# Turning the output weights first, loading them back early, and issuing the middle loop's stores and weight loads from GpSimd

## The chip, the cores and the metric

The kernel runs on one core of one Trainium2 chip. The metric is the device time of one execution in microseconds (us), on the slowest core, which here is the only one.

## The reference, cut to what matters

The program computes a transformer block and all its gradients: `x + A(layernorm(x)) + B(layernorm(x))`, and the vector-Jacobian product for `grad_out`.

```python
def _A_ref(x, mem0, Wq, Wk, Wv, Wo, seg_len):      # S = 2048, D = 512, 32 heads of 128, M = 8, seg = 32
    mem = mem0
    for s in range(n_seg):                         # 64 segments, one after the other
        h = concatenate([mem, xs], axis=1)         # 8 memory rows + 32 rows of the segment
        q, k, v = h @ Wq, h @ Wk, h @ Wv
        o = softmax(mask(q k^T * scale)) v
        o = einsum('bhte,hed->btd', o, Wo)
        mem = o[:, :M, :]                          # the next segment needs this one's output
        ...
def _B_ref(x, w1, b1, w2, b2):                     # F = 1792
    h = x @ w1 + b1
    out = relu(h)**2 @ w2 + b2
```

Because `mem` runs from segment to segment, the kernel has a serial chain of 64 segments forward and a serial chain of 64 segments backward. The backward chain needs the weights transposed: `WoT` (4 MiB), and `WT` for q, k and v (12 MiB).

## The kernel before

The kernel has five stages: the dense part B, the forward chain (to about 1220 us), a **middle loop** of 16 steps, the backward chain, and the weight gradients. The change touches the seam between the two chains.

During the forward chain TensorE (PE) turns two heads of one weight per segment, and a store puts them into scratch in HBM. The order is Wq, Wk, Wv, Wo, so Wo is finished by the last segment.

```python
            t, h0 = divmod(2 * s, H)               # t: 0 = Wq, 1 = Wk, 2 = Wv, 3 = Wo
            def wt():                              # 8 transposes of one step, on PE
                ps["wt"] = fr.tile([P, 8 * P], BF16, name="ps_wt", tag="r")
                ...
            o["ws"] = lambda: dma(S_WOT[...] if t == 3 else S_WT[...], st["wt"][:]...)   # cut
```

At the end of the forward chain the room of Wq, Wk and Wv is freed, and `WoT` is loaded into it. `dma` issues from SyncE (SP), `pdma` from GpSimd. Around it on SP stand the last transposing DMAs of the forward chain and their stores (`OC`, `ON`, `S_ON`).

```python
        def load_back():
            wq_cm.__exit__(None, None, None)
            wk_cm.__exit__(None, None, None)
            ...
            dma(back["WoT"][:], S_WOT[:])          # 4 MiB
```

The middle loop handles the part of the backward pass that does not depend on the chain. One step `b` of it uses loads made a step earlier, and also carries a piece of the dense weight gradients (`ps_w`, from `wA` and `wB`) to keep PE busy. The names with a minus sign belong to the step before.

```python
    LB_ORDER = ("o0mm o1mm qp0- o0ev o1ev qp1- qea0- qeb0- W1- ld o0fl o1fl o0te o1te s0 s1 qea1- qeb1- "
                "d10 d20 d30 d40 so- x0- tu0 d11 d21 d31 d41 tu1 W0 v1- x1- v0").split()
    with sb("ls", 2) as ls, ...:                   # l_gON and the other step tiles have two buffers
            def ld():
                if b + 1 < NB:
                    load(b + 1)                    # l_vTM, l_vTL, l_P, l_kM, l_kL: about 1.1 MiB
                chunk(b + 1)                       # wB: 1 MiB, in runs of 512 bytes
                for t, h in pieces[b:b + 1]:       # 12 pieces, steps 0 to 11
                    dma(WT[t][:, h:h + 8, :], S_WT[:, t, h:h + 8, :])      # 1 MiB
            o["o%dev" % p] = lambda p=p: acp(T["gON"][:, HC[p]], ps["o", p][:])   # ScalarE writes l_gON
            def so():
                dma(S_GOL[b], T["gON"][:])         # this store frees l_gON
                dma(S_GSL[b], T["gS"][:])
                dma(S_GQL[b], T["gq"][:])
        def store(b, i, ps):
            if b < NCH:
                dma(out_9[fc * P:(fc + 1) * P, :], ps["wt", i][:])
            else:
                ...
                    dma(out_7[dc * P:(dc + 1) * P, f0:f0 + CH], ps["wt", i][:, x * CH:(x + 1) * CH])
```

Everything in this excerpt goes through SP's one queue, in this order: loads, `wB`, `WT`, then the stores.

## Time and profile before

| | before |
|---|---|
| time, median of 3 runs | 3210.66 us (3199.31 to 3212.24) |
| profiled execution | 3213.6 us |
| head: start of the last `ps_wt` transposes to the eviction of loop step 1 | 77.3 us |
| loop: eviction of step 1 to that of step 15 | 248.1 us |
| handover: to the first `gv` eviction of the backward chain | 29.9 us |
| backward chain, first to last `gv` eviction | 973.2 us |

"Eviction" is ScalarE's (ACT's) copy of `ps_proj` into `l_gON`; it happens at the same place in every step and makes a good clock.

The first view is part 2 of the profile page of the kernel before: the span in 40 slices of 80.3 us, busy tenths of PE, granted clock of PE, busy tenths of the DMA engines, and the rate (the rows of the other engines are left out).

```profile
PE   7996999999999883657688888888988848999998
PEclk9998999999999996888899999999999978999999
DMA  9447467767677667887468666767766699999993
GB/s 260 161 129 265 142 173 196 197 188 190 169 189 193 166 171 213 233 246 211 124 173 191 162 159 187 171 159 184 183 162 175 164 239 197 216 184 216 187 184 88
```

The dip of PE from the 16th to the 19th slice (3, 6, 5, 7) is the seam. Elsewhere PE stands at 6 tenths or more, apart from a 4 before the last stage, and the change does not reach there.

Next, stretches of the kernel before. Columns: window, its length, busy time of PE, PE's weight loads, VectorE, ACT and GpSimd (with instruction counts), then granted clock, DMA share and GB/s. The first is the loop, the second one step of the backward chain.

```profile
1295.70:1543.80 248.10, 167.73 (x2987) 102.13 (x2996) 66.40 (x154) 53.30 (x125) 0.00 (x0) 0.86 0.80 229
1926.02:1943.98 17.96, 14.75 (x398) 7.35 (x398) 6.77 (x20) 5.44 (x15) 5.11 (x9) 0.90 0.71 234
```

In the loop neither PE (168 of 248 us) nor the DMA engines (0.80) are full. Something makes them wait for each other. The waits of the kernel before between 1280 and 1560 us say what (total us, times, longest):

```profile
PE l_pp L516 <- ACT l_gq L372: 69.7, 15, 14.5
ACT l_gON L372 <- DMA S_GOL<-l_gON: 69.7, 12, 15.4
...
PE ps_w L1024 <- DMA wB<-S_AN: 4.4, 1, 4.4
```

ACT waits 69.7 us for the store that frees `l_gON`, and PE waits as long for a copy queued behind it on ACT. The chain of waits of the kernel before shows why that store is late. Columns: start, length, what.

```profile
1354.94 5.20 PE ps_w L1024 x15
1360.14 0.24 PE ps_tr L165 x4
1360.38 0.16 SPq L1007
1360.54 0.05 issue
1360.59 1.99 SPq L955
1362.58 0.05 issue
1362.63 8.29 DMA S_GOL<-l_gON
...
1371.51 0.59 ACT l_gON L372
```

It reads as a loop. PE's `ps_w` matmuls free `wB`; then SP may issue the next `wB` (L1007) and `WT` (L955); only behind these comes `S_GOL`, and it lands 8.3 us later, though it is only 256 KiB. Then ACT writes `l_gON`, and PE goes on, to the next `ps_w`. So the store waits in two lines: in SP's program, behind an issue that must wait for PE, and in the queue, behind 2 MiB of loads. A step takes 18.6 us on average from step 1 to step 12.

The head has its own stall. The first view is SP's waits between 1220 and 1290 us, the second SP's timeline (start, length of the issue, instruction), both of the kernel before.

```profile
SPq L742 <- DMA S_ON<-OC: 9.5, 1, 9.5
```

```profile
1223.13 1.43 SPq L671 DMA_TRANSPOSE OC<-OT  x1
1224.60 3.44 SPq L530 DMA_DIRECT2D vM<-S_A  x4
1228.14 0.39 SPq L898 DMA_DIRECT2D WoT<-S_WOT  x1
...
1229.25 0.61 SPq L673 DMA_DIRECT2D S_ON<-OC  x1
...
1244.49 1.30 SPq L742 DMA_TRANSPOSE ON<-OTL  x1
```

`S_ON` stands behind the 4 MiB of `WoT`, and the transpose of `ON` must wait for it. A serial row of transposes and stores follows and ends with the first load of `wA` at 1274.1 us.

### The profile page before, as it was taken

Reading aid. Unit: us, or ns where it says so; the run is one execution under the profiler, and the core shown is the slowest. Engines: PE = TensorE matmul, PEld = TensorE weight load, DVE = VectorE, ACT = ScalarE, POOL = GpSimd, SP = SyncE. Lnnn points to the kernel's source line nnn. Section 1 sums busy time; section 2 is a strip of 40 time slices with the busy share of each in tenths; the row PEclk is TensorE's granted clock in tenths of the full one; section 3 lists DMA queues with packets and bytes.
Section 4 is the critical chain, followed back from the end, with each engine's and each line's share of the span. In section 5 each row is a group of like instructions: output and inputs, shape, how many; then the busy total and the mean of one; then the engine's idle time right before and its main releaser. Section 6 shows DMA issues by size and latency. Waiting matters only on the chain.

```text
span 3213.6 us, 115334 instructions
## 1 busy us (share of the span) xinstructions
PE 2726.7 (85%) x51522; PEld 1409.3 (44%) x51672; DVE 1259.6 (39%) x3515; ACT 1011.8 (31%) x2356; POOL 328.5 (10%) x601
## 2 busy tenths in 40 slices
PE   7996999999999883657688888888988848999998
PEld 4453455555544441325444444444444423444443
DVE  5542565655655552222344444444444400100001
ACT  2332454444444441112233333333333201111111
POOL 0000000000000000000122222222222100000000
PEclk9998999999999996888899999999999978999999
DMA  9447467767677667887468666767766699999993
GB/s 260 161 129 265 142 173 196 197 188 190 169 189 193 166 171 213 233 246 211 124 173 191 162 159 187 171 159 184 183 162 175 164 239 197 216 184 216 187 184 88
DMA packets 853923, 594.40 MB, mean 185 GB/s; under 512 B 595745, under 2 KB 735666, under 8 KB 850226
## 3 DMA queue, kind: packets, MB, share of 16 engines
q1 hardware_dynamic: 836018, 532.47, 67.0%
q0 software_dynamic: 17408, 54.54, 5.9%
q8 instruction: 405, 6.64, 0.9%
q14 instruction: 92, 0.75, 0.1%
HBM read 205.14 MB, written 250.10 MB: 142 GB/s over the span
## 4 chain that ended last, share of the span: by engine, by line
PE 58%; DMA 13%; SPq 12%; DVE 6%; ACT 5%; issue 5%; POOL 0%; ACTq 0%; POOLq 0%; DVEq 0%
PE ps_proj L388 12%; PE ps_gR L429 9%; PE ps_gw L1441 8%; SPq L1366 6%; PE b_pp L516 4%; PE ps_sum L438 3%; PE ps_R L429 3%; PE ps_tr L165 2%; DMA S_GOL<-l_gON 2%; DMA out_dram<-wt 2%; PE ps_RL L1145 2%; PE ps_L L346 2%; PE ps_sc L409 1%; PE ps_w L1024 1%; PE f_pp L516 1%
## 5 line engine op out<-in xcount | busy, mean ns | idle before, releaser
L1441 PE MATMUL ps_gw<-gn,HNc 128*128 128x512 bf16 x1881 | 417.4, 381 | 9.0 <-ACT wt L1416 6.9
L1441 PEld LDWEIGHTS <-HNc 128*128 128x128 bf16 x1920 | 188.5, 98 | 233.2 <-issue 11.3
L372 ACT CAST f_N<-ps_proj 128x512 bf16<-128x512 f32 x384 | 218.3, 586 | 183.9 <-PE ps_proj L388 163.3
L1416 ACT CAST wt<-ps_gw 128x512 bf16<-128x512 f32 x126 | 69.2, 592 | 558.3 <-DMA out_dram<-wt 357.5
L388 PEld LDWEIGHTS <-X 128*32 128x32 bf16 x6144 | 159.0, 97 | 171.2 <-issue 16.4
L1399 DVE TENSOR_TENSOR gx<-ps_rows,gb 128x512 f32<-128x512 f32 x16 | 11.1, 691 | 427.3 <-PE ps_rows L1397 427.3
L1441 PE MATMUL ps_gw<-GOc,gn 128*128 128x512 bf16 x627 | 142.0, 386 | 28.5 <-DMA gn<-S_ON 27.7
L429 PE MATMUL ps_gR<-WT,gv 128*32 128x512 bf16 x2048 | 150.4, 387 | 9.7 <-ACT gOT L372 4.4
L429 PE MATMUL ps_gR<-WT,gk 128*32 128x512 bf16 x2048 | 145.6, 405 | 12.2 <-issue 5.3
L429 PE MATMUL ps_gR<-WT,gq 128*32 128x512 bf16 x2048 | 142.2, 404 | 3.7 <-issue 3.7
L388 PE MATMUL ps_proj<-Wk,X 128*32 128x512 bf16 x2048 | 133.5, 393 | 9.7 <-ACT dN L372 4.8
L388 PE MATMUL ps_proj<-Wq,X 128*32 128x512 bf16 x2048 | 130.4, 385 | 7.1 <-DVE X L451 6.5
L388 PE MATMUL ps_proj<-WoT,GT 128*32 128x512 bf16 x2048 | 123.9, 384 | 7.7 <-POOL GT L1175 6.5
L372 ACT CAST gON<-ps_proj 128x512 bf16<-128x512 f32 x128 | 74.9, 585 | 168.9 <-PE ps_proj L388 168.9
L429 PE MATMUL ps_R<-Wo,OT 128*32 128x512 bf16 x2048 | 123.3, 382 | 0.5 <-DVE OT L375 0.4
L388 PE MATMUL ps_proj<-Wv,X 128*32 128x512 bf16 x2048 | 121.5, 378 | 0.0
L438 PE MATMUL ps_sum<-identF,R 128*128 128x128 f32 x512 | 101.7, 299 | 22.4 <-ACT R L372 16.1
L796 POOL COPY kM<-f_kT 128x256 bf16<-128x256 bf16 x64 | 25.6, 401 | 834.7 <-DVE f_kT L375 834.7
L372 ACT CAST gk<-b_pp 128x256 bf16<-128x256 f32 x192 | 65.9, 382 | 142.7 <-PE b_pp L516 134.9
L1441 PEld LDWEIGHTS <-gn 128*128 128x128 bf16 x640 | 63.6, 99 | 105.7 <-DMA gn<-S_ON 28.0
L465 DVE TENSOR_TENSOR ds_t<-ps_sc,l_P 128x256 f32<-128x256 f32 x32 | 12.9, 405 | 216.7 <-PE ps_sc L409 216.7
L438 PEld LDWEIGHTS ps_sum<-identF,R 128*128 128x128 f32 x512 | 56.5, 144 | 84.4 <-ACT R L372 59.1
(229 smaller groups left out, 4849.4 us busy)
## 6 DMA issues: line engine op xcount, KB each, us to landing
S_A<-f_N SPq DMA_DIRECT2D x64, 512.0 KB
out_dram<-wt SPq DMA_DIRECT2D x142, 128.0 KB
S_A<-f_N SPq DMA_DIRECT2D x64, 256.0 KB
S_ON<-OC SPq DMA_DIRECT2D x64, 256.0 KB
b_qN<-S_A POOLq DMA_DIRECT2D x64, 256.0 KB, 3.9
b_kN<-S_A POOLq DMA_DIRECT2D x64, 256.0 KB, 3.8
S_GB<-gv SPq DMA_DIRECT2D x32, 512.0 KB
S_GB<-gq SPq DMA_DIRECT2D x32, 512.0 KB
```

What stands on the lines that cost most here:

```text
L165: nc.tensor.transpose(ps_ap, in_ap, ident[base:base + k, base:base + k])
L346: nc.tensor.matmul(ps[:], lhsT=x(dc), rhs=Wqkv[t][:, dc, c0:c0 + 512], start=(dc == 0), stop=(dc == DC - 1))
L372: nc.scalar.copy(out, in_)
L388: nc.tensor.matmul(ps[32 * g:32 * g + 32, :], lhsT=hT[:, dc, :], rhs=W[:, dc, c:c + 4 * P], start=(dc == 0), stop=(dc == DC - 1), tile_pos ...
L409: nc.tensor.matmul(sc3[32 * g:32 * g + 32, k, c:c + n], lhsT=qT[:, 4 * h + k, g, :], rhs=kT[:, 4 * h + k, g, :], start=(mask is None), sto ...
L429: nc.tensor.matmul(R[32 * g:32 * g + 32, :], lhsT=XT(k, g), rhs=W[:, g * KH + k, :], start=(first and k == 4 * h), stop=(last and k == 4 * ...
L438: nc.tensor.transpose(st["T"][:, c * P:(c + 1) * P], R4()[:, c * P:(c + 1) * P], identF[:])
L516: nc.tensor.matmul(o, lhsT=N_[32 * g:32 * g + m, kk * P:(kk + 1) * P], rhs=X(kk)[32 * g:32 * g + m], start=(i == 0), stop=(i == len(jobs) ...
L1145: nc.tensor.matmul(ps["R", i][32 * g:32 * g + 32, :], lhsT=B_[n][:, k, g, :], rhs=W[:, g * KH + k, :], start=(ps["n", i] == 1 and m == 0), ...
L1366: nc.sync.dma_start_transpose(t_[:, b, :].rearrange("p (k e) -> p k e", k=KH), blocks(b)[:, g].rearrange("p k r -> p (k r)"))
L1416: nc.any.tensor_copy(wt[:], ps[:])
L1441: nc.tensor.matmul(ps[:], lhsT=l(rc), rhs=r(rc), start=(n == 0), stop=(n == RC_ALL - 1))
```

## The change

The intent has two parts. First, Wo is turned at the beginning of the forward chain rather than at the end. Its last store is then long done, `WoT` can be loaded as soon as the last reader of Wq, Wk and Wv is done, and it goes out on GpSimd's queue, off SP's. Second, the stores of the middle loop and the `WT` pieces also move to GpSimd's queue.

```diff
-    def play(order, n, steps, lefts, step, blk, last={}):
+    def play(order, n, steps, lefts, step, blk, done=None):
...
                         steps[step(s)][k]()
+                        if done and s == NSEG - 1:
+                            done(k)
...
             t, h0 = divmod(2 * s, H)
+            t = (3, 2, 1, 0)[t]
...
-            dma(back["WoT"][:], S_WOT[:])
+            pdma(back["WoT"][:], S_WOT[:])
...
+            reads = {"wt"} | {"%s%dmm" % (x, p) for x in "qkv" for p in (0, 1)}
+            def done(k):                      # load_back() after the last of these in the last segment
...
                 for t, h in pieces[b:b + 1]:
-                    dma(WT[t][:, h:h + 8, :], S_WT[:, t, h:h + 8, :])
+                    pdma(WT[t][:, h:h + 8, :], S_WT[:, t, h:h + 8, :])
...
             def so():
-                dma(S_GOL[b], T["gON"][:])
-                dma(S_GSL[b], T["gS"][:])
-                dma(S_GQL[b], T["gq"][:])
+                pdma(S_GOL[b], T["gON"][:])
+                pdma(S_GSL[b], T["gS"][:])
+                pdma(S_GQL[b], T["gq"][:])
...
-                dma(out_9[fc * P:(fc + 1) * P, :], ps["wt", i][:])
+                pdma(out_9[fc * P:(fc + 1) * P, :], ps["wt", i][:])
...
-                    dma(out_7[dc * P:(dc + 1) * P, f0:f0 + CH], ps["wt", i][:, x * CH:(x + 1) * CH])
+                    pdma(out_7[dc * P:(dc + 1) * P, f0:f0 + CH], ps["wt", i][:, x * CH:(x + 1) * CH])
```

PE, VectorE and ACT get the same instructions (the turned weights come in another order). DMA issues move from SP to GpSimd: stores, 12 `WT` pieces and `WoT`. No byte is added or removed.

More of the change, by code (lines that the diff above doesn't have):

```diff
@@ L561, in play @@
                         lefts[blk(b)][k[2:]]()
-                        if b == NB - 1 and k in last:
-                            last.pop(k)()
                 else:
@@ L908 @@
             steps[0]["ld0"]()
+            reads = {"wt"} | {"%s%dmm" % (x, p) for x in "qkv" for p in (0, 1)}
+            def done(k):
+                if k in reads:
+                    reads.discard(k)
+                    if not reads:
+                        load_back()
             for n in range(-1, NB + 4):
-                play(F_ORDER, n, steps, lefts, lambda s: s, lambda b: b, {"L.lm": load_back} if n > 0 else {})
+                play(F_ORDER, n, steps, lefts, lambda s: s, lambda b: b, done)
     xl_cm.__exit__(None, None, None)
```

## The prediction

> **What bounds the kernel now.** Over the whole span PE is busy 85% (page, part 1), so only a stretch where PE is not the limit can give much. The slices (part 2) show one: PE drops to 3 to 8 tenths around 1220 to 1570 us, between the forward and the backward chain. Busy time by stretch: 1200-1300 PE 42.5 of 100 us; 1300-1500 PE about 34 of every 50 us, granted clock 0.73 to 0.89, DMA share 0.78 to 0.86 at 228 to 244 GB/s.
>
> Two parts:
>
> 1. Head, 1220-1288 us. SP issues the 4 MB load of WoT at 1228.1. It must follow the last S_WOT store (1222.5), because Wo is turned last. DMA runs at 339 to 349 GB/s until 1244, and the S_ON store issued behind it at 1229.3 lands only then: SP waits 9.5 us (SP's waits: L742 on S_ON). After that a serial chain of transposes and stores, about 3 + 2 us each, runs to 1272, then the first wA/wB load to 1288.
> 2. Middle loop, 16 steps, 1288-1557. The chain of waits repeats: PE frees wB, SP issues wB and WT (1 MB each), and behind them S_GOL, which lands 7 to 9 us later; only then may ACT write l_gON again. ACT waits 69.7 us for S_GOL; PE waits 69.7 us for the l_gq copy queued behind it on ACT. The evictions are 18.6 us apart on average from step 1 to step 12. The last steps, which do not wait, take 12.1 us: PE's own time at full clock.
>
> **What the change does.** No arithmetic is added; the order of the engines' instructions shows only that the transposes of Wo, Wv, Wk, Wq come in the reverse order. SP loses 88 issues, GpSimd gains 88.
> - WoT no longer waits for a late store; GpSimd can issue it when Wk's last reader is done (about 1212). Two WT pieces follow at once. S_ON no longer sits behind 4 MB. Gain about 7 us of the 9.5; contention with the vM loads at 1224 takes the rest. The serial chain to 1288 stays.
> - The loop's stores no longer wait for wB's issue; the l_gON wait on S_GOL should go to near 0. GpSimd pays about 0.54 us per issue (its DMAs in the backward chain), some 4 us a step: hidden.
> - Bytes stay. The Trainium skill ("DMA: Bandwidth & Descriptors", section "Issuing engines are not separate DMA queues") says several issuing engines share the same 16 DMA engines. So the next limit of a step with a WT piece is bytes: about 4.2 MB (WT 1, wB 1, loads 1.1, stores 0.6, outputs 0.25 MiB). Estimate at about 295 GB/s (between 244 here and 345 for WoT): 14.3 us. Steps without WT become PE-bound, 12.2 us.
>
> Sum: steps 1 to 12, 204.6 us to about 157 (two pieces are prefetched); later steps 44 to 37; head 7; handover to the backward chain about 3 (SP has no stores ahead of its first loads). About 64 us, all on the critical path. The forward chain, backward chain and last stage should not move.
>
> **Predicted: 3147 us, 3120 to 3180.** Faster by over 2%: 0.49; within: 0.49; slower: 0.02.
>
> **What would show it.** WoT issued on GpSimd before 1222; SP's L742 wait under 2 us; ACT's wait on S_GOL under 10 us; eviction spacing 13.5 to 15 us in WT steps and about 12.2 in later ones; DMA above 280 GB/s in the loop; clock nearer 0.95.
>
> **What would make it wrong.** Two queues reach 340 GB/s: the loop is PE-bound at 12.2 us and the time near 3120. Or the GpSimd queue delivers no more than 250 GB/s, wB then arrives late (a new PE wait on wB), and the time is near 3175. Or the early 6 MB delay vM and the last forward block.

## The result, and the profile after

The median is 3166.79 us over 4 runs (3156.69 to 3174.08), against 3209.71 for the kernel before (4 runs: the three above and one more of 3208.76). The ratio is 0.987, with a 95% interval of 0.9835 to 0.9905: a gain, but within 2%. All outputs are right. Ratios here are the mean time of one kernel's runs over that of the other's runs of the same rounds, so they are not quite the ratio of the medians that are quoted.

| stretch, us | before | after | difference | predicted |
|---|---|---|---|---|
| up to the last `ps_wt` | 1218.4 | 1219.4 | +1.0 | 0 |
| head | 77.3 | 78.7 | +1.4 | -7 |
| loop, steps 1 to 12 | 204.5 | 176.9 | -27.6 | -48 |
| loop, steps 12 to 15 | 43.6 | 37.2 | -6.4 | -7 |
| handover | 29.9 | 29.9 | 0.0 | -3 |
| backward chain | 973.2 | 954.6 | -18.6 | 0 |
| last stage | 666.7 | 669.0 | +2.3 | 0 |
| span of the profile | 3213.6 | 3165.7 | -47.9 | -64 |

So the total is short of the prediction by some 20 us, and one of the gains, in the backward chain, was not predicted at all. Part 2 of the page of the kernel after, the same rows, in slices of 79.1 us:

```profile
PE   7996999999999884568688888988888649999998
PEclk9998999999999997889899999999999979999999
DMA  9437466756667667999468667767776799999993
GB/s 265 162 119 273 135 182 187 201 167 191 192 172 191 180 175 221 225 277 259 116 176 185 162 173 193 168 171 190 175 167 188 176 232 193 219 185 216 182 185 85
```

PE's dip (4, 5, 6, 8) is a little less deep, and the DMA engines now read 9 in three slices where they read 8, 8 and 7. The stretches of the kernel after, loop and one backward step:

```profile
1298.10:1512.20 214.10, 160.17 (x2987) 98.72 (x2996) 66.52 (x154) 54.39 (x126) 45.85 (x86) 0.89 1.05 255
1893.28:1908.55 15.27, 13.08 (x398) 6.89 (x398) 6.77 (x20) 5.45 (x16) 5.10 (x9) 1.00 0.84 274
```

The loop runs at 255 GB/s, not at 295. (The DMA share is the summed time of all packets over that of 16 engines; it can read above 1.) GpSimd's 86 issues there take 0.53 us each, 46 us in all, hidden as predicted. The same 2987 matmuls took PE 7.6 us less, at a higher granted clock. The Trainium skill ("TensorE: Matmul & The Clock Gate", section "HAM oscillation — how this bites in real kernels") describes this coupling, a PE that waits for DMA loses its clock; the records agree in direction, 0.86 before and 0.89 after. The two backward steps hold the same 398 matmuls; one ran at clock 0.90 in 17.96 us, the other at 1.00 in 15.27. That is a first hint at what the 18.6 us of the backward chain are.

The waits of the kernel after between 1280 and 1560 us:

```profile
PE l_pp L516 <- ACT l_gq L372: 20.0, 14, 11.4
...
PE ps_w L1038 <- DMA wB<-S_GH1N: 15.5, 3, 11.8
...
ACT l_gON L372 <- DMA S_GOL<-l_gON: 11.5, 1, 11.5
...
PE ps_w L1032 <- DMA wB<-S_AN: 9.5, 2, 5.2
```

The old wait is down from 69.7 to 11.5 us, all of it in one step. A new one is there: PE waits 25.0 us for `wB` (15.5 + 9.5), against 4.4 before. The chain of waits of the kernel after passes through the 11.5 us wait:

```profile
1323.12 0.54 POOL out_dram L1060
1323.65 0.52 POOL WT L963
1324.17 22.44 DMA S_GOL<-l_gON
...
1347.20 0.59 ACT l_gON L372
```

`S_GOL` is issued right behind a 1 MiB `WT` piece again, now on GpSimd's queue, and takes 22.4 us. The queue alone does not make that number: in the same order, the store lands in 8.2 to 9.8 us in six of the seven other steps with a `WT` piece whose landing the trace has. The next views, in the columns of the stretches, are step 3 of the kernel after (eviction 3 to eviction 4), 12 us inside it, and 12 us of step 3 of `e2`, an experiment below with the same order of `WT` and stores.

```profile
1322.80:1346.70 23.90, 12.10 (x246) 6.01 (x241) 4.76 (x12) 3.93 (x9) 5.10 (x10) 0.86 1.11 187
1328.00:1340.00 12.00, 7.80 (x155) 3.85 (x155) 4.74 (x11) 2.21 (x5) 2.14 (x4) 0.99 1.02 100
```

```profile
1330.00:1342.00 12.00, 8.97 (x165) 4.44 (x162) 4.74 (x11) 2.76 (x7) 2.88 (x7) 0.88 1.09 295
```

For 12 us the DMA engines read as busy (share 1.02) and moved 100 GB/s, where `e2` moved 295. This slow stretch stands at the same place in both repeats of the kernel after (`e8` and `e11` below: 143 and 80 GB/s over 12 us, and `S_GOL` landing after 18.6 and 23.7 us), and none of the other eleven profiles has 12 us of the loop below 140 GB/s at a share near 1. What causes it is not shown.

The steps of the loop are uneven: 12.4 us where nothing waits, which is PE's own time, but 23.9, 22.9 and 26.3 us in three of them. The first is the slow stretch. The other two stand around the 2 MiB load of `wA`, where every version has long steps.

In the head, the timelines of SP and of GpSimd of the kernel after:

```profile
1223.73 7.68 SPq L671 DMA_TRANSPOSE OC<-OT  x1
1231.45 4.68 SPq L530 DMA_DIRECT2D vM<-S_A  x4
...
1246.81 1.29 SPq L742 DMA_TRANSPOSE ON<-OTL  x1
```

```profile
1220.32 0.70 POOL L899 DMA_DIRECT2D WoT<-S_WOT  x1 [6.68 <-PE ps_wt L165]
1221.02 1.05 POOL L963 DMA_DIRECT2D WT<-S_WT  x2
```

`WoT` went out at 1220.3 us, 8 us earlier than before, and the 9.5 us wait of L742 is gone. Still `ON` came no sooner: 27.4 us after the last `ps_wt`, against 26.1. Issuing the transpose of `OC` now took 7.68 us instead of 1.43, the `vM` loads behind it went out 7 us later, and the time was lost again before `S_ON` was issued at 1241.6.

### The profile page after: what moved, and what is told of

It reads as the page before. It is cut to its first block, busy times and chain, and to the rows that moved or that the text cites. A ratio compares the mean times of both kernels' runs of the same rounds, so it can differ in the third digit from the quotient of the medians.

```text
span 3165.7 us, 115378 instructions
## 1 busy us (share of the span) xinstructions
PE 2708.3 (86%) x51522; PEld 1404.0 (44%) x51672; DVE 1258.9 (40%) x3515; ACT 1013.1 (32%) x2356; POOL 383.3 (12%) x704
## 4 chain that ended last, share of the span: by engine, by line
PE 58%; DMA 12%; SPq 11%; DVE 7%; ACT 5%; issue 5%; POOL 0%; ACTq 0%; POOLq 0%; DVEq 0%
PE ps_proj L388 12%; PE ps_gR L429 9%; PE ps_gw L1449 8%; SPq L1374 5%; PE b_pp L516 4%; PE ps_sum L438 3%; PE ps_R L429 3%; PE ps_tr L165 2%; PE ps_RL L1153 2%; DMA out_dram<-wt 2%; PE ps_L L346 2%; DMA vM<-S_A 2%; PE ps_B L295 1%; PE ps_sc L409 1%; PE ps_gxb L304 1%
## 5 line engine op out<-in xcount | busy, mean ns | idle before, releaser
L438 PE MATMUL ps_sum<-identF,R 128*128 128x128 f32 x512 | 100.7, 296 | 22.1 <-ACT R L372 15.8
L375 DVE COPY R<-ps_gR 128x256 f32<-128x256 f32 x64 | 27.2, 425 | 151.4 <-ACT R L372 111.1
```

Of the source, the lines that this page charges most:

```text
L438: nc.tensor.transpose(st["T"][:, c * P:(c + 1) * P], R4()[:, c * P:(c + 1) * P], identF[:])
```

## The experiments

My first theory had three parts. The gain comes from the loop's stores leaving the queue of the loads. The loop is then held by the bytes, at a lower rate than I had taken. The head gains nothing because 6 MiB in flight slow down what stands beside them. The rivals: the gain comes from `WT` having a queue of its own; the loop is held by the order on GpSimd's queue; the 18.6 us of the backward chain are a real effect of the change.

### How well do the same kernels repeat?

`e1_before_again` and `e10_before_third` are the kernel before, unchanged; `e8_after_again` and `e11_after_third` are the kernel after, unchanged. The diffs are empty. `e10` and `e11` ran on the same chip.

> The kernel before, unchanged, profiled once more. The two profiles differ by 18.6 us in the backward chain (first to last eviction of gv: 973.2 us before, 954.6 us after), which the change does not touch. Theory (chance): some of its 64 steps run at a granted clock of 0.90 and take about 18 us in place of 15, and their number varies from run to run; so this profile gives a backward chain other than 973 by 5 us or more, anywhere from 950 to 985. Rival (the change causes it): 973 within 4 us again.

> The kernel after, unchanged, on the same chip. Theory: its total lies 0 to 8 us above the run with the stores alone (ratio to before 0.985 to 0.990), its head (last ps_wt to step 1) takes 78 to 79 us again, the loop (step 1 to 15) 203 to 215 us with at least one long wait for S_GOL or wB, and the backward chain something between 955 and 982 us by chance, not 954.6 again. Rival (the 18.6 us in the backward chain come from the change): 958 or less.

> The kernel before once more, beside the kernel after on the same chip, to compare their backward chains on one chip. Theory (chance): 962 to 982 us, with 10 to 15 steps at a clock of 0.90; and within 10 us of the kernel after of this call.

> The kernel after once more. Theory (chance): backward chain within 10 us of the kernel before of this call. Rival: 15 us or more below it, as in the first pair of profiles. Head (last ps_wt to step 1) 78 to 80 us and steps 1 to 15 in 205 to 216 us for the third time.

Measured: `e1` 3212.24 us (single run; the kernel before beside it 3221.17, median of 7). `e8` 3150.94 against 3201.59 (7 runs), ratio 0.9842 (0.9807 to 0.9876). `e10` 3215.72 and `e11` 3173.74, single runs, beside 3215.25 (9 runs).

| stretch, us | before | e1 | e10 | after | e8 | e11 |
|---|---|---|---|---|---|---|
| head | 77.3 | 77.5 | 77.0 | 78.7 | 79.0 | 80.9 |
| loop | 248.1 | 245.0 | 251.6 | 214.1 | 212.1 | 211.1 |
| handover | 29.9 | 29.2 | 29.7 | 29.9 | 28.5 | 28.6 |
| backward chain | 973.2 | 968.8 | 965.7 | 954.6 | 965.1 | 966.3 |
| its steps at clock 0.90 | 13 | 12 | 10 | 7 | 14 | 10 |

What follows: the loop's gain and the head's small loss repeat in every pair. The backward chain's gain does not. `e10` and `e11` spend 965.7 and 966.3 us there, with ten slow steps each. In the first pair 13 steps ran at the lower clock in one profile and 7 in the other; at about 2.7 us a step (17.96 less 15.27) that makes 16 of the 18.6 us, an estimate. What varies by chance is their number; their places do not vary much: the fourth step is slow in all 14 profiles, and most of the others fall at the same few places. What sets the clock there is not shown. With three profiles of each kernel (965.7 to 973.2 us before, 954.6 to 966.3 after), an effect of a few us is not excluded. In the same-chip pair the sum is -42.1 us, of which the loop is -40.5, the head +3.9, and the rest small.

### Each part of the change alone

These three ran in one call; the kernel before beside them had a median of 3221.17 us (7 runs). `e2_queues_only` keeps the old order of the weights and the old load of `WoT`. As in the full change, its first two `WT` pieces go out before the loop (at 1222.0 and 1222.7 us), ahead of `WoT` (1237.6):

```diff
-                    dma(WT[t][:, h:h + 8, :], S_WT[:, t, h:h + 8, :])
+                    pdma(WT[t][:, h:h + 8, :], S_WT[:, t, h:h + 8, :])
-                dma(S_GOL[b], T["gON"][:])      # likewise S_GSL, S_GQL, out_9, out_7
+                pdma(S_GOL[b], T["gON"][:])
```

> Only the loop's stores and the WT loads on the GpSimd queue; WoT as in the kernel before. Theory: the whole gain comes from the loop, so evictions of l_gON from step 1 to step 12 take 175 to 185 us (before 204.6, after 176.9), the head keeps its length within 4 us (eviction of step 1 near 1296 to 1300), total 3165 to 3185. Rival (the early WoT is part of the gain): total above 3190.

`e3_order_only` turns Wo first and loads `WoT` early from GpSimd, and leaves the loop as it was:

```diff
+            t = (3, 2, 1, 0)[t]
-            dma(back["WoT"][:], S_WOT[:])
+            pdma(back["WoT"][:], S_WOT[:])      # called when the last reader is done, as in the change
```

> Only Wo turned first and WoT loaded early on the GpSimd queue; the loop as before. Theory: the early 4 MB delay the vM loads, which the last forward block waits for, by about what the freed S_ON store gains: step 1 of the loop starts within 4 us of before (1295.7), the loop still takes 200 to 209 us from step 1 to 12, total 3200 to 3215. Rival (my prediction): the head is 7 us shorter, total 3200 or less with step 1 at 1289.

`e4_stores_only` moves the stores of the loop and nothing else:

```diff
-                dma(S_GOL[b], T["gON"][:])      # likewise S_GSL, S_GQL, out_9, out_7
+                pdma(S_GOL[b], T["gON"][:])
```

> Only the loop's stores on the GpSimd queue; WT stays behind wB on SP's queue. Theory (the loop is now bound by the bytes of all transfers, about 258 GB/s): step 1 to step 12 takes 175 to 190 us, as in the kernel after (176.9). Rival (arbitration: WT on a ring of its own takes bandwidth from the urgent wB): it is faster than the kernel after, under 168 us.

| | time, us | ratio (95%) | head | loop steps 1 to 12 | loop |
|---|---|---|---|---|---|
| e2, queues | 3177.56 | 0.9872 (0.9844 to 0.9900) | 78.9 | 163.8 | 206.9 |
| e3, order | 3219.73 | 1.0003 (0.9983 to 1.0023) | 74.0 | 198.5 | 242.2 |
| e4, stores | 3173.89 | 0.9845 (0.9815 to 0.9874) | 77.8 | 160.6 | 203.2 |

The order alone is worth nothing within 0.2%. The stores alone give the whole gain. Moving `WT` as well gives no more: the loop is 3.7 us longer in `e2` than in `e4`, although `e2` has 2 MiB of `WT` loaded before the loop. One profile of each cannot settle 3.7 us: the loop of one kernel varies by 3.0 us (after) and 6.6 us (before) in three profiles. In the three profiles of the full change it is 8 to 11 us longer than in `e4`, and 4 to 7 longer than in `e2`; the slow stretch of step 3 is what they have and `e2` has not. Without those 12 us the loop of the kernel after has 264 GB/s (worked out from 255 over 214.1 us and 100 over 12), beside 267 in `e2`. The median times do not show it: 0.9872 for `e2`, 0.987 and 0.9842 for the full change.

Both `e2` and `e4` were faster in steps 1 to 12 than I had expected. `e4`, with 160.6 us, was within what the rival allowed, but `e2` has `WT` on GpSimd's queue and took 163.8, so the rival's reason is not shown. The stretch of the loop in `e4`, in the columns of the stretches above:

```profile
1302.50:1505.70 203.20, 160.34 (x3000) 98.65 (x2996) 66.54 (x154) 54.60 (x126) 40.51 (x76) 0.93 1.05 280
```

Here the rate is 280 GB/s, with the same bytes as before (280 times 203.2 is 56.9 MB; before, 229 times 248.1 is 56.8). The next views are from the waits of `e4` from 1280 to 1560 us (the first was 69.7 us before; the list holds no wait of ACT for `S_GOL` any more), and its line for that store in the list of DMA issues (KiB each, median us to landing), followed by that of the kernel after.

```profile
PE ps_w L1030 <- DMA wB<-S_GH1N: 14.0, 4, 8.3
...
PE ps_w L1024 <- DMA wB<-S_AN: 9.9, 5, 4.5
...
PE l_pp L516 <- ACT l_gq L372: 9.3, 14, 0.7
```

The new wait for `wB` is here too, 23.9 us (14.0 + 9.9), almost as in the kernel after. So `WT` on GpSimd's queue is not what brings it.

```profile
S_GOL<-l_gON POOLq DMA_DIRECT2D x16, 256.0 KB, 6.4
```

```profile
S_GOL<-l_gON POOLq DMA_DIRECT2D x16, 256.0 KB, 8.7
```

The store lands in 6.4 us with `WT` on SP and in 8.7 us behind `WT` on GpSimd. The Trainium skill ("DMA: Bandwidth & Descriptors", section "Queues, rings and completion order") says that each DMA engine takes turns between queues packet by packet. Of the queues of SP and ACT it also says that each engine takes descriptors in ring order. The numbers agree with both, if the order holds for GpSimd's queue too: a store on a queue of its own gets its turn, a store behind 1 MiB on its own queue waits for it.

Of the two lines in which the store stood before, the one in SP's program was the longer. In the median of steps 1 to 10, `S_GOL` was issued 9.8 us after the next eviction in the kernel before, and 0.5 us after it in `e4`; its landing went from some 8 us to 6.4.

In `e3` the head became 3.0 to 3.5 us shorter than in the three profiles of before, half of the 7 that the prediction had: more than nothing, less than the rival. `S_ON` could go out 17 us after the last `ps_wt`, against 22 in the kernel after, and 11 before (where it then landed late, behind `WoT`). One transposing issue on SP took 6.46 us there. With the two `WT` pieces in flight as well (the full change) even these 3 us are gone. The time of `e3` does not show such a small gain.

### Longer runs, and a later start of WoT

These ran with `e8`; the kernel before had a median of 3201.59 us (7 runs). `e5_stores_rows8k` is `e4`, with the scratch of `wB` laid out so that one partition reads 8 KiB in one run instead of 16 runs of 512 bytes:

```diff
-    S_AN = dram.tile([S, F], BF16, name="S_AN")                         # S_GH1N likewise
+    S_AN = dram.tile([F // (2 * P), P, TC, 2 * P], BF16, name="S_AN")
-                    dma(dstD[rr0:rr0 + P, :], Nt[:])
+                    dma(dstD[:, :, rr0 // P, :].rearrange("n p f -> p n f"), Nt[:].rearrange("p (n f) -> p n f", f=2 * P))
-                rows_in(part[b][:], (S_GH1N if second else S_AN)[:, n * CH:(n + 1) * CH])
+                dma(part[b][:], (S_GH1N if second else S_AN)[n])
```

> The loop's stores on the GpSimd queue (the run with the stores alone), and the wB chunks laid out in DRAM so that each partition reads one run of 8 KB in place of 16 pieces of 512 B; same bytes. What still stops PE in that run is wB (the chain of waits holds nine waits for wB of 7 to 16 us). Theory (the small pieces make the transfers slow): step 1 to step 15 falls from 203 to 180 to 192 us, total 10 to 20 us below the run with the stores alone; the first stage (0 to 300 us) may lose up to 5 us to smaller stores. Rival (bytes alone set the rate): step 1 to 15 stays at 198 to 208, total the same or worse.

`e6_stores_gate` is `e4`, with `WoT` on GpSimd's queue behind a small copy that waits for `ON`, so that the transfer starts only when the chain of `ON` no longer needs the engines:

```diff
+                if b == NB - 1:                                    # in otr(), after the transpose of ON
+                    nc.gpsimd.tensor_copy(gate[:], st["ON"][:, 0, 0:1])
+                    load_back()
-            dma(back["WoT"][:], S_WOT[:])
+            pdma(back["WoT"][:], S_WOT[:])
```

> The loop's stores on the GpSimd queue, and WoT on the GpSimd queue but held until the last block's ON has landed, so that it is neither ahead of the vM loads nor ahead of the S_ON store. Theory (in the head the 4 MB cost time wherever they stand before that chain, and DMA idles after it): the last ps_wt to step 1 of the loop takes 67 to 72 us (77 to 78 before, 74.0 with the early load alone), total about 8 us below the run with the stores alone. Rival (the serial chain of transposes and stores after it slows by as much): 75 us or more, total unchanged.

`e7_rows8k_gate` has both edits.

> Both of the above. If the gains are independent, its total is below the run with the stores alone by the sum of the two, 18 to 28 us, which is 60 to 75 us below the kernel before.

| | time, us | ratio (95%) | head | loop |
|---|---|---|---|---|
| e5, stores + long runs | 3147.88 | 0.9811 (0.9777 to 0.9846) | 77.0 | 198.5 |
| e6, stores + gate | 3171.02 | 0.9883 (0.9845 to 0.9922) | 90.8 | 201.1 |
| e7, both | 3157.41 | 0.9864 (0.9826 to 0.9902) | 76.8 | 191.7 |

`e5`: the rate rose from 280 to 289 GB/s and the loop fell by 4.7 us, less than the 11 to 23 us expected, to 198.5, inside the rival's range of 198 to 208. One profile of each hardly resolves such a difference. The length of the runs is at most a small part of what keeps the rate down. The feared loss in the first stage did not show: the first eviction of the forward chain stands at 306.5 us, at 306.2 in `e4`. The kernel after (`e8`) had 3150.94 us.

`e6`: my theory of the head failed here. `ON` did come early, 14.7 us after the last `ps_wt` instead of 26.1, and yet the head of this profile became 13 us longer. SP's timeline of `e6`, with the same transposing DMA of `OC` that took 1.25 us to issue before:

```profile
1239.32 1.30 SPq L743 DMA_TRANSPOSE ON<-OTL  x1
...
1246.87 24.82 SPq L672 DMA_TRANSPOSE OC<-OT  x1
```

A transposing DMA whose issue fell into the 4 MiB transfer on GpSimd's queue held SP for 24.82 us. The transfer itself was slow here too: `WoT` took 31.3 us to land (14.6 in `e8`, 14.7 in `e3`, 15.8 in `e7`), and from 1258 to 1272 us all DMA together moved 64 GB/s, another slow stretch. Which of the two held up the other is not shown, and `e7`, with the same edit, has no such stretch in its head. In the kernel after the issue took 7.68 us (6.63 and 6.36 in its repeats), in `e3` 6.46, in `e7` 7.87 us. In the kernel before the same transposes took at most 1.43 us, but none of them was issued while `WoT` was in flight, because the wait of L742 kept them back. The Trainium skill ("DMA: Bandwidth & Descriptors", section "Rules for kernel authors") says that a transpose next to ordinary DMAs "needs nothing". That is said of correctness, and the results were indeed correct; it is not free in time. What holds SP is not shown by these traces; only the coincidence is, in four different kernels. It is not a matter of transposes or of GpSimd's queue alone: right behind `wA` and `wB`, both on SP, an ordinary load took 6.14 us to issue in the kernel before.

`e7`: the two edits did not add up. It came out 44 us below the kernel before, not 60 to 75. The head's loss was absent (76.8 us) and the loop was the shortest yet with `WT` inside it, but the timed runs came out no better than those of `e5`.

### Are the bytes of WT what holds the loop?

`e9_wt_after_loop` is `e4` with the 12 loads of `WT` taken out of the loop and issued on SP behind it:

```diff
-                for t, h in pieces[b:b + 1]:
-                    dma(WT[t][:, h:h + 8, :], S_WT[:, t, h:h + 8, :])
...
+            for t, h in pieces:                        # after the loop
+                dma(WT[t][:, h:h + 8, :], S_WT[:, t, h:h + 8, :])
```

> A diagnosis, not an improvement: the loop's stores on the GpSimd queue, and all twelve WT loads (12 MB) taken out of the loop and issued behind it. Theory (bytes limit the loop once the store is out of the way): with 12 of about 56 MB gone, step 1 to step 15 falls from 203 us (stores alone) to 175 to 188 us, most steps at 12.4 us, and the time to the first gv eviction grows by about 36 us (12 MB at 345 GB/s). Rival (wB is late because it is issued late, one step ahead, whatever else is in flight): step 1 to 15 stays above 195 us.

Measured: 3157.38 us, a single run, beside 3215.25 (9 runs). The loop took 183.0 us, as expected. The handover took 44.2 us instead of 29.6, so 14.6 more rather than the 36 expected: more of the loads was hidden than I had thought. The stretch of the loop in `e9`:

```profile
1295.30:1478.30 183.00, 153.40 (x2987) 96.62 (x2996) 66.54 (x154) 54.50 (x125) 40.52 (x76) 0.95 0.98 248
```

With `WT` gone, every step took 12.3 to 12.6 us, PE's own time, apart from the three around the 2 MiB load of `wA` (15.8, 8.7 and 22.1 us). Those 12 MiB cost about 20 us of the loop. As moving them to another queue (`e2`) did not remove that cost, their bytes are the likelier cause than their place in a queue. Note the DMA share: it is 0.98 here, where PE is the limit, and 1.05 in `e4`, where it is not. A share near 1 alone would not have told these two apart.

### WoT in parts

`e12_wot_parts` is `e5`, with `WoT` on SP in four parts of 1 MiB, one after each transposing DMA of the serial row:

```diff
-            dma(back["WoT"][:], S_WOT[:])
+        def load_part(b, c):
+            if b == NB - 1:
+                dma(back["WoT"][:, c, :], S_WOT[:, c, :])
+                load_part(b, 0)                        # after the transpose of ON
+                    if g < 3:
+                        load_part(b, g + 1)            # after the transposes of OC
```

> Candidate for a better version: stores on the GpSimd queue, wB in runs of 8 KB, Wo turned last as in the kernel before, and WoT on SP's queue in four parts of 1 MB, each behind one of the last transposes, so that SP does not wait for a store behind 4 MB and the parts fill the pauses of the serial chain. Theory: last ps_wt to step 1 takes 70 to 74 us (77 before, 77.0 in the run with the stores and 8 KB runs), total 3 to 7 us below that run, so a ratio to the kernel before of about 0.978 to 0.981. Rival (each part delays the chain by its own 3 us): 77 us or more, ratio 0.981 or above.

Measured: 3155.06 us over 5 runs (3147.56 to 3165.91) against 3215.25, ratio 0.9813 (0.9787 to 0.9838). The head took 73.5 us, as expected, 3.5 to 4 less than before. The transposes of `ON` and `OC` between the parts took 1.24 to 1.30 us to issue. The total is no better than that of `e5`, and the ratio of 0.9813 falls on the rival's side of 0.981; a gain of 4 us is a tenth of a per cent and below what these runs resolve.

`e5` (0.9811) and `e12` (0.9813) lean better than the change (0.987 and 0.9842), but the intervals overlap; that they beat it is not shown. One further idea, to load `wA` a step earlier into a second buffer, did not fit into the memory left, by my count; it was not built, and no run shows it.

## Why the prediction was right or wrong

**The range and the class were right, the middle was not.** The prediction was 3147 us, 3120 to 3180; the result is 3166.79. It gave "within 2%" a chance of 0.49, and that came true; "faster by over 2%" had the same chance, so this says little. The gain was 43 us where 64 were predicted.

**What bounds the seam: right.** The wait for `S_GOL` behind `wB` and `WT` on SP's queue was the limit. `e4` moves only the stores, and ACT's wait for `S_GOL` falls from 69.7 us to none in the list. The prediction said "near 0" and "under 10 us" for the change; it was 11.5, because of the next point.

**The step that failed most is the loop's term, "steps 1 to 12, 204.6 us to about 157", through "Estimate at about 295 GB/s".** Measured were 176.9 us (173.8 and 171.6 in the repeats), at 255 GB/s. The shortfall of 15 to 20 us has two parts. `e2`, which makes the same change to the loop, took 163.8 us at 267 GB/s, so some 7 us are the rate, taken too high. Of the other 8 to 13 us, 4 to 9 are in step 3 (23.9, 20.1 and 25.2 us, against 15.8 in `e2`), with the slow stretch that only the full change shows: all DMA at 80 to 143 GB/s for 12 us, `S_GOL` behind `WT` landing after 18.6 to 23.7 us, and ACT waiting for it. No term of the prediction stood for such a stretch, and its cause stays open. I had also put the stores and the `WT` pieces into one group, as if it made no difference what shares a queue with what. `e4`, with `WT` on SP, took 160.6 us at 280 GB/s; that it is better than `e2` is not shown. The warning in the prediction, "wB then arrives late (a new PE wait on wB), and the time is near 3175", names a symptom that came (4.4 to 25.0 us), but its reason, GpSimd's queue, is not needed for it: `e4` has 23.9 us of it with `WT` on SP's queue.

**"Later steps 44 to 37": right.** They took 37.2 us, at 12.4 us a step (38.3 and 39.5 in the repeats).

**"Head 7": wrong, even in its sign.** The head lost 1.4 to 3.9 us. The predicted mechanism did work, L742's wait went from 9.5 us to none, and `WoT` was out before 1222 us. What failed is "contention with the vM loads takes the rest": the early transfer of 6 MiB held the transposing issue in front of `vM` for 7.68 us, and `S_ON` went out 22 us after the last `ps_wt` instead of 11. That gave back all that the removed wait had won. `e3`, with 4 MiB, keeps 3 us; `e6` shows a stall of 24.8 us, in a slow stretch; `e12`, in which only parts of 1 MiB stand beside the transposes, gets 3.5 to 4 us.

**"Handover about 3": wrong and small.** It was 0 in the first pair and 1.1 us in the pair on one chip.

**"The backward chain should not move": right, though the first pair of profiles says otherwise.** Of its 18.6 us some 16 are the different number of slow steps (an estimate), and the pair of the same call has no difference (965.7 and 966.3).

**The citation in the prediction.** The Trainium skill ("DMA: Bandwidth & Descriptors", section "Issuing engines are not separate DMA queues") says that several issuing engines share the 16 DMA engines and that using several "will only save the time on the sequencer". The first half agrees: the bytes remained, and they became the limit. The second half does not hold in this case. `e4` saves 45 us in the loop with the same bytes. The 76 issues that left SP in that stretch took 0.38 to 0.43 us each in a step of the kernel before, an estimate of 30 us for all of them, but only eight of them, 3.3 us in all, are steps of the chain of waits in the loop; it has the wait for PE in SP's program and some 8 us for a store to land. What was saved is mostly waiting in line.

## What to carry to other kernels

A small store that frees a buffer should not stand behind large prefetches on one queue, and above all not behind an issue that must wait for the engine that the store will release; give it another queue. Here nothing was won by moving the prefetches along (`e2` against `e4`), and the store then took 8.3 us to land in `e2` instead of 6.4 in `e4`, in the median. Where a transfer takes much longer than its neighbours, look at the rate of all DMA in that stretch before blaming the queue. When a wait is removed in front of a serial chain, ask what the earlier transfer will run beside: here a transfer of 4 to 6 MiB went together with stalls of 6 to 25 us in the issue of the transposing DMAs of that chain. Before believing a difference in a stretch that the change does not touch, repeat both kernels on one chip and compare the granted clock step by step.

## What the Trainium skill lacked or had wrong

- "DMA: Bandwidth & Descriptors", section "Issuing engines are not separate DMA queues": a second issuing engine saves more than issue time when a store stands behind loads. `e4` moved 90 stores and cut the loop from 248.1 to 203.2 us with the same 57 MB. The section does not mention this.
- The same page has no time cost for a transposing DMA beside a large transfer from GpSimd; its section "Rules for kernel authors" has only that nothing is needed. The issue took 6.4 to 24.8 us in four kernels instead of 1.2 to 1.4; the highest figure fell into a slow stretch.
- The rates of the same page's section "Bandwidth" are those of loads by themselves. For a mix of loads and stores of 64 KiB to 2 MiB on two queues the runs show 255 to 258 GB/s in the full change, 267 in `e2`, 280 with `WT` on SP's queue, and 289 with runs of 8 KiB for `wB`, the last three from one profile each.
- No page has a cause that I could match to the slow stretches: 80 to 143 GB/s for 12 us at a DMA share of 1.0 to 1.1 in step 3 of the full change, three times of three, and 64 GB/s for 14 us in `e6`.
- In "TensorE: Matmul & The Clock Gate" I found no figure, beyond the warm-up at a kernel's start, for how the granted clock of a single busy core varies from run to run: 7 to 14 of the backward chain's 63 steps ran at clock 0.90 (18.0 us instead of 15.3 in the pair shown), in profiles of two kernels.
